# Shared products of the end blocks on 64 or on 128 rows of the array

## The chip, the cores and the metric

The kernel runs on one core of a Trainium2 chip. Its time is the device time of one execution in microseconds (us); a lower time is better. The core has five engines that run side by side and wait for each other through semaphores: TensorE (PE in the profile, its weight loads PEld), VectorE (DVE), ScalarE (ACT), GpSimd (POOL) and SyncE (SP). DMA queues move data between device memory and the on-chip memory. TensorE multiplies a stationary operand, loaded as weights, with a moving operand that streams through its array of 128 rows by 128 columns. It can also be used as smaller arrays: a product named 64*32 in the profile uses 64 rows and 32 columns, one named 64*128 uses 64 rows and all columns, and one named 128*128 uses the whole array.

## The reference

The first part is attention with a block mask, for 4 batches, 8 heads, 768 tokens of 64 values, in blocks of 32 tokens (24 blocks). The second part is a feed-forward network on the attention's output.

```python
scores = scale * np.matmul(q, k.transpose(0, 1, 3, 2))
mask = np.abs(blk_i - blk_j) <= window                  # window = 1
mask = mask | (blk_i == 0) | (blk_j == 0) | (blk_i == n_blocks - 1) | (blk_j == n_blocks - 1)
for qb in range(n_blocks):
    for kb in sampled_blocks[qb]:                       # 3 random blocks
        mask[qb * block:(qb + 1) * block, kb * block:(kb + 1) * block] = True
scores = np.where(mask, scores, -1000000000.0)
attn = softmax(scores)
x = np.matmul(attn, v)                                  # to [3072 tokens, 512]
h = x @ w_in                                            # [3072, 2048]
out = gelu(h) @ w_out                                   # [3072, 512]
```

So a block of queries sees its own block and its two neighbours, three sampled blocks, and the two end blocks (block 0 and block 23). Query blocks 0 and 23 see all blocks; they are called dense here. All other query blocks need the values of both end blocks, each weighted with its own probabilities.

## The kernel before

The kernel works through eight units, two for each batch (`Unit`, L300). A unit holds three quads of four query blocks. The first unit of a batch (quads 1, 2, 0) holds also the two dense blocks; the second one (quads 3, 4, 5) has only sparse blocks. Quads 0 and 5 have three sparse blocks, since their fourth is dense; the other two groups of a unit have four.

All work is written out in one order by hand (`manual_schedule`), and every engine runs its instructions in that order. For each unit there is a stage for the first feed-forward product (`ffn1_step`, L502), and after it an attention stage for the next unit (`attention`, L562) into which the pieces of the second feed-forward product of the unit before are put as filling (`ffn2_pieces`, L524, L529; the lists of numbers that are given to `attention` say how many pieces go into which round). In a round of the attention stage the order is: scores on TensorE (`scores`, L335), row maxima on VectorE (L360 for sparse, L363 for dense blocks), exponentials on ScalarE (L377, L381), a transpose of the probabilities in 32x32 squares on VectorE (`turned`, L394 into the tile pT, L399 into ptd), and when a group is done, the weighed values on TensorE (`values`, L407), the division by the sums on VectorE (`divided`, L467), a transpose on TensorE (`outputs`, L486, tile tx) and a copy to the feed-forward input xT on ScalarE (L494).

On the on-chip memory's partitions the eight heads stand in pairs: rows 0 to 63 hold two heads and rows 64 to 127 two others, in each of two groups G. `values` works for one half (one G) at a time. In the tile kv a block's values stand with 32 rows for a head, so that one product over 64 rows adds two heads at once; each head has its own 65 columns (64 values and a one that gives the sum), and the columns of the other head of the pair hold zeros. The two pairs h = 0 and h = 1 go to two places of the accumulator av.

For a group of four query blocks a half has 52 products. The first four are the shared products of the end blocks (L434 and L457): the weights are the probabilities of all four query blocks (128 columns) for the end block, the moving operand is the end block's values (130 columns), once for the rows 0 to 63 and once for the rows 64 to 127, first for block 0 and then for block 23. They are 64*128 products. The other 48 are of one query block each (64*32): own block, neighbours and sampled blocks, whose values were gathered into gb beforehand (`gather`, L296). The weights wait for pT from VectorE.

The gathers for the next unit run during the first feed-forward stage. For a new batch they are on VectorE (L739 to L741), then comes a hold on POOL (`hold_loads`, L158: a copy of one value that makes POOL wait) and the rest of the gathers on POOL. For the first batch's second unit the hold stands at L719. `value_list` (L191) works out once, in three scratch rows of 72 numbers, which sampled blocks count.

Of the kernel before, what the change touches and what calls it, by code (L numbers as in the profile page):

```python
# [10 lines left out]
F32 = mybir.dt.float32  # L11
BF16 = mybir.dt.bfloat16
# [8 lines left out]
def kernel(  # L21
# [58 lines left out]
    ptd = const.tile([P, 2, NE, 2, BL, 2], BF16, name="ptd")  # L80
    xTs = [const.tile([P, KIN, UT], BF16, name=f"xT{i}") for i in range(2)]
    g = const.tile([P, KOUT, UT], BF16, name="g")
    mark = const.tile([1, 1], BF16, name="mark")
    junk = const.tile([1, 1], BF16, name="junk")

# [9 lines left out]
    def sampled(i, r):  # L95
        c0 = GW * (i // 3) + 4 * BW + DW * (i % 3) + BW * r
        return gb[:, c0:c0 + BW]
# [58 lines left out]
    def hold_loads(x):  # L156

        nc.gpsimd.tensor_copy(mark, x)  # L158
# [30 lines left out]
    vf = const.tile([1, NB, NR], I32, name="vf")  # L189

    def value_list():  # L191
        rf = const.tile([1, NB, NR], F32, name="rf")
        inv = const.tile([1, NB, NR], F32, name="inv")
        tmp = const.tile([1, NB, NR], F32, name="tmp")
        nc.vector.tensor_copy(rf, raw[:, :, :, 0])
        nc.vector.tensor_tensor(tmp, rf, jrow, op=ALU.subtract)
        nc.vector.tensor_tensor(tmp, tmp, tmp, op=ALU.mult)
        nc.vector.tensor_scalar(inv, tmp, 1.0, None, op0=ALU.is_le)
        for c in (0.0, float(NB - 1)):
            nc.vector.scalar_tensor_tensor(out=inv, in0=rf, scalar=c, in1=inv,  # L200
                                           op0=ALU.is_equal, op1=ALU.max)
        for a, c in ((1, 0), (2, 1)):
            w = NR - a if c == 0 else 1
            nc.vector.tensor_tensor(tmp[:, :, 0:w], rf[:, :, a:a + w],
                                    rf[:, :, c:c + 1].to_broadcast([1, NB, w]), op=ALU.is_equal)
            nc.vector.tensor_tensor(inv[:, :, a:a + w], inv[:, :, a:a + w], tmp[:, :, 0:w],
                                    op=ALU.max)
        nc.vector.scalar_tensor_tensor(out=vf, in0=inv, scalar=float(NB), in1=rf,
                                       op0=ALU.mult, op1=ALU.max)
# [56 lines left out]
    def gather_fixed(kT, place, copy=None, part=None):  # L266

        copy = copy or nc.vector.tensor_copy
        groups = gb.rearrange("p (g x) -> p g x", x=GW)
        js = sorted(place)  # L270
        runs = [[j for j in js if place[j] - j == c] for c in sorted({place[j] - j for j in js})]
        for run in runs if part != 1 else ():
            i0 = place[run[0]]
            assert i0 % 3 == 0
            for lane in range(min(3, len(run))):
                m, g0 = len(range(lane, len(run), 3)), i0 // 3
                c0, j = BW + KC * lane, run[0] + lane - 1
                copy(
                    groups[:, g0:g0 + m, c0:c0 + 3 * BW].rearrange("p g (w c) -> p g w c", c=BW)[:, :, :, 0:KC],
                    kT[:, j:j + 3 * m, :].rearrange("p (g w) c -> p g w c", w=3))  # L280
        if part == 0:
            return
        at = slice(min(place.values()) // 3, max(place.values()) // 3 + 1)
        n = at.stop - at.start
        copy(groups[:, at, 0:3 * KC].rearrange("p g (l c) -> p g l c", c=KC),
             kT[:, None, 0:1, :].to_broadcast([P, n, 3, KC]))
        copy(  # L287
            groups[:, at, 4 * BW:GW].rearrange("p g (l x) -> p g l x", x=DW)[:, :, :, NR * BW:DW],
            kT[:, None, NB - 1:NB, :].to_broadcast([P, n, 3, KC]))

    def gather(unit, js, at, c0=0, c1=BW, engine=None):

# [114 lines left out]
    def values(unit, grp, half):  # L407
        kv = kvs[unit.b % 2]
        if half == 0:

            pool, tag = (psA, "A") if grp == units[0].ends[len(units[0].rounds) - 1] else (psV, "V")
            st[grp, "av"] = pool.tile([P, 2, 512], F32, name="av", tag=tag)
        av = st[grp, "av"]
        if grp[0][0] == "d":
            pv = ptd.rearrange("p g c x q e -> p g c (x q) e")
            for c in range(NB // 2 * half, NB // 2 * (half + 1)):
                for G in range(2):
                    for h in range(2):
                        rows = slice(64 * h, 64 * h + 64)
                        c0 = KC + V2 * G  # L420
                        nc.tensor.matmul(av[64 * G:64 * G + 64, h, 0:V2],
                                         lhsT=pv[rows, G, c // 2, :, c % 2],
                                         rhs=kv[rows, c, c0:c0 + V2],
                                         start=(c == 0), stop=(c == NB - 1))
            n, m = 4, 2
        else:
            slots = [j for rnd in grp for j in rnd[1]]
            G = half
            c0 = KC + V2 * G
            pv = st[grp, "pt"][:, G].rearrange("p c (q e) -> p c q e", e=2)  # L430

            work = []
            if len(slots) == 4:
                work += [(0, 4, c, kv[:, blk, c0:c0 + V2]) for c, blk in ((0, 0), (7, NB - 1))]  # L434
            for c in range(1, 7) if work else range(8):
                for s, j in enumerate(slots):
                    if c in (0, 7):
                        blk = 0 if c == 0 else NB - 1
                        if abs(blk - j) <= 1:
                            continue  # L440
                        src = kv[:, blk, c0:c0 + V2]
                    elif c < 4:
                        src = kv[:, j - 2 + c, c0:c0 + V2]
                    else:
                        src = sampled(unit.place[j], c - 4)[:, c0:c0 + V2]
                    work.append((s, 1, c, src))
            fresh, left = set(range(len(slots))), {s: 0 for s in range(len(slots))}
            for s, w, _, _ in work:
                for x in range(s, s + w):
                    left[x] += 1  # L450
            for s, w, c, src in work:
                at = range(s, s + w)
                for x in at:
                    left[x] -= 1
                for h in range(2):
                    rows = slice(64 * h, 64 * h + 64)
                    nc.tensor.matmul(av[32 * s:32 * (s + w), h, V2 * G:V2 * G + V2],  # L457
                                     lhsT=pv[rows, c % 4, BL * s:BL * (s + w), c // 4], rhs=src[rows],
                                     start=s in fresh, stop=left[s] == 0)
                fresh -= set(at)  # L460
            n, m = len(slots), 4
            if half:
                st.pop((grp, "pt"))
        if half:
            st[grp, "av"] = av, n, m
# [237 lines left out]
    for n, unit in enumerate(units):  # L703
# [11 lines left out]
        for s in range(KOUT // 2):  # L715
            ffn1_step(n, 2 * s)
            if s == 0:
                if n == 0:
                    hold_loads(sampled(nxt.place[J1[7]], NR - 1)[0:1, BW - 1:BW])  # L719
                    gather(nxt, J1[8:], others, engine=nc.gpsimd)  # L720
                    ones(1)
                elif fresh and b + 2 < B:
                    xT, t0 = column[b, unit.groups[-2][0]]
                    hold_loads(xT[0:1, 0, t0:t0 + 1])
                    load_by_token(qn, q, b + 2)
                    load_by_token(kn, k, b + 2)
                    turn_queries(b + 2)
                elif nxt is not None and not fresh:
                    if b + 1 < B:
                        turn_keys()  # L730
                        hold_loads(sampled(nxt.place[J1[7]], NR - 1)[0:1, BW - 1:BW])
                        load_values(b + 1)
                    gather(nxt, J1[8:], others, engine=nc.gpsimd)
            if s == 7 and nxt is not None:
                table(AF.Exp)
                if n > 0 and not fresh and b + 1 < B:
                    next_keys(b + 1)
            if fresh and s == 0:
                gather_fixed(keys(b + 1), nxt.place)  # L739
                gather(nxt, J0[3:9], known)  # L740
                gather(nxt, J0[:3], known)  # L741
                hold_loads(sampled(nxt.place[J0[2]], NR - 1)[0:1, BW - 1:BW])
                gather(nxt, J0[9:], others, engine=nc.gpsimd)
        filler = ffn2_pieces(n)
# [51 lines left out]
```

## Time and profile before

| what | value |
|---|---|
| time, median of 3 runs | 290.33 us (289.07 to 290.67) |
| span of the profiled execution | 288.1 us |
| TensorE busy in the span | 263.8 us (92%) |
| VectorE, ScalarE busy | 207.6 us, 207.7 us (72% each) |
| GpSimd busy | 101.2 us (35%) |
| share of TensorE in the chain that ended last | 65% |
| second feed-forward product, L529 | 336 products, 87.0 us busy |
| first feed-forward product, L507 | 512 products, 85.0 us busy |
| weighed values, L457 | 2400 products, of which 128 are shared ones of the end blocks |

The profile is of one execution, and its time as the runs count it isn't given beside its span; the median of the runs is 2.2 us above the span. Busy time of TensorE counts a product from its issue to its last result, so products that follow each other overlap, and a group's mean is a latency. What a product costs in a row of products is the distance from one start to the next. The timeline gives starts to 0.01 us; a row there joins instructions of one kind that follow each other, and the count behind its x covers those of the window that was asked for. In a row with several products the last one starts at the row's end less the latency of one.

### The profile page before, as it was taken

To read this page: it belongs to the slowest core of one execution; us is meant where nothing else is said; L and a number is where in the kernel's file an instruction comes from. 1 tells how busy PE (TensorE), PEld (TensorE's weight loads), DVE (VectorE), ACT (ScalarE), POOL (GpSimd) and SP (SyncE) were. 2 spreads that over 40 slices of the span, in tenths; PEclk is the share of its full clock that TensorE was granted. 3 is DMA by queue.
4 is the path that set the end of the run, shared out by engine and by line. 5 is a ranking of instruction groups with operands and counts; after the bars stand their busy time and mean duration, and the time that the engine had idled before them with its cause. 6 is when DMAs were issued, how large, how long until landed. Compare 5 with 4: busy or idle time off the path is not lost.

```text
span 288.1 us, 11491 instructions
## 1 busy us (share of the span) xinstructions
PE 263.8 (92%) x4918; PEld 143.4 (50%) x4918; DVE 207.6 (72%) x476; ACT 207.7 (72%) x379; POOL 101.2 (35%) x209
## 2 busy tenths in 40 slices
PE   1798799998998999999998999899999999899994
PEld 1624555445553555445544556355535555356543
DVE  7599787866888967598998876798749796871000
ACT  8779746875868966796778865986688766966611
POOL 8788944308792001920990004900120032000000
PEclk9999999999999999999999999999999999999999
DMA  6997399919999116991997119930101110111002
GB/s 103 168 91 118 50 197 205 206 49 113 91 165 151 39 41 149 81 69 41 102 151 116 65 51 134 84 50 35 40 0 41 39 41 0 39 42 39 0 36 74
DMA packets 72981, 23.80 MB, mean 83 GB/s; under 512 B 63073, under 2 KB 69474, under 8 KB 72930
## 3 DMA queue, kind: packets, MB, share of 16 engines
q0 software_dynamic: 56912, 13.64, 77.8%
q1 hardware_dynamic: 16018, 9.44, 11.9%
q8 instruction: 38, 0.62, 0.9%
q14 instruction: 13, 0.11, 0.2%
HBM read 27.26 MB, written 6.29 MB: 116 GB/s over the span
## 4 chain that ended last, share of the span: by engine, by line
PE 65%; ACT 19%; DVE 7%; issue 3%; DMA 3%; POOL 1%; ACTq 0%; POOLq 0%
PE hp L507 27%; PE op L529 18%; PE av L457 10%; ACT pp L377 8%; ACT L405 4%; PE sc L335 3%; ACT g L510 3%; DMA qn<-in_q_dram 3%; DVE nm L360 3%; PE tx L486 2%; PE av L558 2%; PE op L558 2%; ACT pp L381 2%; PE pt L227 2%; DVE nm L363 1%
## 5 line engine op out<-in xcount | busy, mean ns | idle before, releaser
L529 PE MATMUL op<-w_out_sb,g 128*128 128x512 bf16 x336 | 87.0, 381 | 0.5 <-ACT os L515 0.3
L507 PE MATMUL hp<-xT,w_in_sb 128*128 128x384 bf16 x512 | 85.0, 326 | 0.8 <-ACT xT L494 0.4
L377 ACT ACTIVATE pp<-sc,nm 128x256 bf16<-128x256 f32 x176 | 75.3, 542 | 7.7 <-DVE nm L360 7.5
L510 ACT ACTIVATE g<-hp 128x768 bf16<-128x768 f32 (+1 forms) x72 | 52.1, 738 | 31.4 <-PE hp L507 31.4
L507 PEld LDWEIGHTS <-w_in_sb 128*128 128x128 bf16 x512 | 50.0, 98 | 36.0 <-issue 3.1
L360 DVE TENSOR_REDUCE nm<-sc 128x4 f32<-128x1024 f32 (+1 forms) x48 | 52.9, 1107 | 7.2 <-PE sc L335 7.2
L296 POOL COPY gb<-kv 128x388 bf16 (+1 forms) x87 | 36.5, 474 | 26.5 <-DVE gb L287 24.1
L529 PEld LDWEIGHTS <-g 128*128 128x128 bf16 x336 | 28.2, 97 | 34.6 <-issue 11.6
L296 DVE COPY gb<-kv 128x388 bf16 x177 | 39.9, 305 | 1.2 <-DMA qn<-in_q_dram 1.2
L457 PEld LDWEIGHTS <-pT 64*32 64x32 bf16 (+1 forms) x2400 | 26.1, 91 | 19.8 <-DVE pT L394 7.9
L394 DVE STREAM_TRANSPOSE pT<-pp 128x512 f32<-128x512 f32 (+1 forms) x48 | 31.5, 656 | 5.9 <-ACT pp L377 5.7
L457 PE MATMUL av<-kv,pT 64*32 64x130 bf16 (+1 forms) x1344 | 28.2, 220 | 3.0 <-DVE pT L394 1.1
L158 POOL COPY mark<-gb 1x1 bf16<-1x1 bf16 x6 | 1.1, 178 | 80.2 <-DVE gb L296 80.2
L335 PE MATMUL sc<-gb,qT 64*32 64x256 bf16 x704 | 19.1, 274 | 5.7 <-ACT pp L377 3.7
L134 POOL DMA_DIRECT2D kv<-in_v_dram x32 | 22.9, 724 | 1.8 <-DMA qn<-in_q_dram 1.1
L494 ACT COPY xT<-tx 128x512 bf16<-128x512 bf16 (+1 forms) x32 | 13.6, 450 | 13.1 <-PE tx L486 13.1
L335 PEld LDWEIGHTS <-qT 64*32 64x32 bf16 x832 | 11.2, 90 | 21.4 <-issue 14.6
L381 ACT ACTIVATE pp<-sc,nm 128x768 bf16<-128x768 f32 x16 | 17.1, 1104 | 4.9 <-DVE nm L363 4.9
L363 DVE TENSOR_REDUCE nm<-sc 128x1 f32<-128x768 f32 x16 | 15.0, 944 | 7.8 <-PE sc L335 7.3
L457 PE MATMUL av<-gb,pT 64*32 64x130 bf16 x1056 | 19.8, 220 | 0.7 <-issue 0.7
L405 ACT ACT_TABLE_LOAD x15 | 19.2, 1283 | 0.3
L476 DVE TENSOR_TENSOR xh<-av,rec 128x512 bf16<-128x512 f32 (+2 forms) x28 | 18.3, 652 | 1.0
(75 smaller groups left out, 225.3 us busy)
## 6 DMA issues: line engine op xcount, KB each, us to landing
out_dram<-os SPq DMA_DIRECT2D x23, 256.0 KB, 2.0
kv<-in_v_dram POOLq DMA_DIRECT2D x32, 96.0 KB, 6.5
w_out_sb<-in_moe_w_out_dram POOLq DMA_DIRECT2D x2, 1024.0 KB, 13.4
kn<-in_k_dram POOLq DMA_DIRECT2D x4, 384.0 KB, 11.2
qn<-in_q_dram POOLq DMA_DIRECT2D x4, 384.0 KB, 12.8
qn<-in_q_dram POOLq DMA_DIRECT2D x12, 128.0 KB, 5.4
kn<-in_k_dram POOLq DMA_DIRECT2D x12, 128.0 KB, 5.9
w_in_sb<-in_moe_w_in_dram POOLq DMA_DIRECT2D x2, 512.0 KB, 10.2
```

Source lines behind the costliest of these rows:

```text
L134: nc.gpsimd.dma_start(out=kvs[b % 2][32 * hh:32 * hh + 32, 0:NB, c0:c0 + D], in_=v[b, h].rearrange("(n p) d -> p n d", p=BL))
L296: (engine or nc.vector).tensor_copy(sampled(unit.place[j], r)[:, None, c0:c1], src[:, bass.ds(at[j][r], 1), :])
L335: nc.tensor.matmul(o, lhsT=qT[rows, j // 4, pr, BL * (j % 4):BL * (j % 4) + BL], rhs=rhs(rows, pr), start=True, stop=True)
L360: nc.vector.tensor_reduce(out=nm[:, 0:2 * n].rearrange("p (g j) -> p g j", g=2), in_=A4[:, :, 0:n, :], op=ALU.max, axis=AX.X, negate=True)
L377: nc.scalar.activation(at[:, x // n, x % n], A[:, a:a + 256].rearrange("p (e c k) -> p e c k", e=2, k=BL), AF.Exp, bias=nm[:, x:x + 1])
L381: nc.scalar.activation(pp[:, 0:S].rearrange("p (c k e) -> p c e k", e=2, k=BL), A[:, 0:S].rearrange("p (c e k) -> p c e k", e=2, k=BL), AF ...
L394: nc.vector.transpose(pt.rearrange("p g c x -> p (g c) x")[:, :, 64 * s:64 * (s + n)].bitcast(F32), pp[:, 0:512 * n].bitcast(F32).rearrang ...
L405: nc.scalar.activation(junk, zero[0:1, 0:1], func)
L457: nc.tensor.matmul(av[32 * s:32 * (s + w), h, V2 * G:V2 * G + V2], lhsT=pv[rows, c % 4, BL * s:BL * (s + w), c // 4], rhs=src[rows], start ...
L507: nc.tensor.matmul(hp[:, i, 0:T], lhsT=w_in_sb[:, ki, (m + i) * P:(m + i + 1) * P], rhs=xTs[n % 2][:, ki, 0:T], start=(ki == 0), stop=(ki ...
L510: nc.scalar.activation(g[:, m + i[0]:m + i[1], 0:T], hp[:, i[0]:i[1], 0:T], AF.Gelu)
L529: nc.tensor.matmul(op, lhsT=g[:, m, t * P:(t + 1) * P], rhs=w_out_sb[:, m, :], start=(m == 0), stop=(m == KOUT - 1))
```

## The change

The shared products of the end blocks keep their weights and their number, but each one uses all 128 rows. For that a new tile `ends` holds the values of the two end blocks twice: in its first copy the rows 64 to 127 are zero, in its second the rows 0 to 63. A product with the first copy adds the pair h = 0 alone, one with the second copy the pair h = 1. The four products of a half are 128*128 products with 130 columns, in the same order as before. The first unit keeps the old form.

The tile is filled by `apart`: two copies of 64 rows for a batch. For the first batch POOL does them ahead of the hold in the first feed-forward stage of unit 0, with two memsets that write the zeros once; for the three other batches VectorE does them behind the gathers of the new batch. The three scratch rows of `value_list` get no tiles of their own any more and lie in the tile g, which is first written later.

```diff
+    ends = const.tile([P, 2, 2, 2 * V2], BF16, name="ends")
...
-        rf = const.tile([1, NB, NR], F32, name="rf")
-        inv = const.tile([1, NB, NR], F32, name="inv")
-        tmp = const.tile([1, NB, NR], F32, name="tmp")
+        rf, inv, tmp = [g[0:1, i, 0:2 * NB * NR].bitcast(F32).rearrange("o (j r) -> o j r", r=NR)
+                        for i in range(3)]
...
+    def apart(b, engine):
+        for h in range(2):
+            rows = slice(64 * h, 64 * h + 64)
+            engine.tensor_copy(ends[rows, h], kvs[b % 2][rows, 0:NB:NB - 1, KC:BW])
...
-            if len(slots) == 4:
+            if len(slots) == 4 and unit is not units[0]:
+                for i, c in enumerate((0, 7)):
+                    for h in range(2):
+                        nc.tensor.matmul(av[:, h, V2 * G:V2 * G + V2],
+                                         lhsT=pv[:, c % 4, 0:P, c // 4],
+                                         rhs=ends[:, h, i, V2 * G:V2 * G + V2],
+                                         start=(i == 0), stop=False)
+            elif len(slots) == 4:
                 work += [(0, 4, c, kv[:, blk, c0:c0 + V2]) for c, blk in ((0, 0), (7, NB - 1))]
-            for c in range(1, 7) if work else range(8):
+            for c in range(1, 7) if len(slots) == 4 else range(8):
...
-            fresh, left = set(range(len(slots))), {s: 0 for s in range(len(slots))}
+            shared = len(slots) == 4 and unit is not units[0]
+            fresh = set() if shared else set(range(len(slots)))
+            left = {s: 0 for s in range(len(slots))}
...
                 if n == 0:
+                    for h in range(2):
+                        nc.gpsimd.memset(ends[64 * h:64 * h + 64, 1 - h], 0.0)
+                    apart(0, nc.gpsimd)
                     hold_loads(sampled(nxt.place[J1[7]], NR - 1)[0:1, BW - 1:BW])
...
                 gather(nxt, J0[:3], known)
+                apart(b + 1, nc.vector)
                 hold_loads(sampled(nxt.place[J0[2]], NR - 1)[0:1, BW - 1:BW])
```

## The prediction

> **What bounds the kernel now.** I read the page first (span and busy shares), then the stretches of the attention stages, then the groups kept apart by shape, then the timeline around single products.
>
> ```profile
> span 288.1 us, 11491 instructions
> ...
> PE 263.8 (92%) x4918; PEld 143.4 (50%) x4918; DVE 207.6 (72%) x476; ACT 207.7 (72%) x379; POOL 101.2 (35%) x209
> ```
>
> The runs of before have a median of 290.33 us (289.07 to 290.67); the profiled execution spans 288.1, so some 2.2 us lie around the span, and I leave them as they are. The next view has one row for each stretch in which an attention stage has its weighed values (us, then busy time and instructions of PE, PEld, DVE, ACT, POOL, then the granted clock).
>
> ```profile
> 94.75:107.98 13.23, 13.21 (x387) 7.36 (x388) 10.67 (x24) 10.00 (x24) 0.00 (x0) 1.00 0.12 43
> 124.10:137.30 13.20, 13.19 (x399) 7.12 (x399) 11.90 (x22) 10.20 (x20) 0.58 (x2) 1.00 0.45 52
> 157.35:170.59 13.24, 13.22 (x387) 7.37 (x388) 10.66 (x24) 10.02 (x24) 0.00 (x0) 1.00 0.12 44
> ```
>
> TensorE is busy 13.21 of 13.23 us: in these stages TensorE's own order is the path, and a nanosecond added to or taken from it is a nanosecond of the result. The clock is 1.00, so nothing here is about throttling. The dense stage (first row) comes back as the third: the schedule repeats, so one stage can stand for three.
>
> **The products that change.** All shared products of the end blocks are this group; 32 halves of four products each.
>
> ```profile
> L457 PE MATMUL av<-kv,pT 64*128 64x130 bf16 x128 | 9.2, 223 | 1.1 <-DVE pT L394 1.1
> ```
>
> The four halves of the first unit keep the old form, so 28 halves (112 products) change. The 223 ns is the latency of one, not what one costs. The cost is in the starts, here of a half that follows another half:
>
> ```profile
> 101.49 0.42 PE L457 MATMUL av<-gb,pT 64*32 64x130 bf16 x24
> ...
> 101.85 0.29 PE L457 MATMUL av<-kv,pT 64*128 64x130 bf16 x4
> ...
> 102.07 0.36 PE L457 MATMUL av<-kv,pT 64*32 64x130 bf16 x22
> ```
>
> From the first shared product to the first small one (64*32) pass 0.22 us. Next, what full-array products (128*128) cost. The tx products have 128 columns, ours 130.
>
> ```profile
> 103.91 0.39 PE L486 MATMUL tx<-identity,xh 128*128 128x128 bf16 x4
> ...
> 104.13 0.59 PE L529 MATMUL op<-w_out_sb,g 128*128 128x512 bf16 x2
> ```
>
> ```profile
> 98.21 0.28 PE L486 MATMUL tx<-identity,xh 128*128 128x128 bf16 x2
> ...
> 98.41 0.47 PE L457 MATMUL av<-kv,pT 64*128 64x130 bf16 x12
> ```
>
> Four tx products and the step into the next product of the same shape take 0.22, so 0.055 a step, each with its own weight load. Two tx products and the step into another shape take 0.20: 0.09 more than two steps. So a change of shape costs 0.09 us. This is where the old form loses: 0.22 is one step for a pair, one step for the second pair, and 0.09 to the small shape; four products in two steps means that the two row halves run at once.
>
> The new form does the four one behind the other: 4 x 0.056 (130 columns for 128) and 0.09 to the small shape, 0.32. Against 0.22 that is 0.10 more for each half, **28 x 0.10 = +2.7 us** (2.7 to 2.8 by the rounding of the rows), wherever the half stands. The Trainium skill, "TensorE: Matmul & The Clock Gate", section "Why this matters for your kernels", speaks against this change in the same sense: a product with few rows takes as long as one with 128, and the gain of short ones is that they run beside each other. By that rule the padding buys nothing in the array; the trace agrees (0.22 for four short products with the exit, 0.22 for four full ones without it).
>
> **What is saved is the way in.** Behind a full-array product the shape no longer changes. The FFN steps and one such entry:
>
> ```profile
> 272.89 3.45 PE op L558 x16
> ```
>
> ```profile
> 124.95 0.81 PE L529 MATMUL op<-w_out_sb,g 128*128 128x512 bf16 x3
> 125.69 0.40 PEld L457 LDWEIGHTS <-pT 64*128 64x128 bf16 x25 [0.42 <-issue]
> ```
>
> Sixteen FFN products in 3.45 are 0.216 a step. The third product of the row at 124.95 starts at 125.38, and the shared one starts with its load at 125.69: 0.31, so 0.095 can go. Over the 28 halves the timeline has 18 behind an FFN product (first 56.90, last 255.44), 6 behind tx products (first 65.91, last 223.61) and 4 behind small products (101.85, 164.45, 227.05, 256.19). The last four save nothing. If the other 24 saved all, the gain would be 24 x 0.094 = 2.3 us, and the whole +0.5.
>
> They don't save all, since the product must also have its weights, pT, from VectorE's transpose.
>
> ```profile
> 95.56 0.70 DVE L394 STREAM_TRANSPOSE pT<-pp 128x512 f32<-128x512 f32 x1
> ...
> 96.35 0.34 PEld L457 LDWEIGHTS <-pT 64*128 64x128 bf16 x14 [0.42 <-DVE pT L394]
> ```
>
> ```profile
> 100.33 0.70 DVE L394 STREAM_TRANSPOSE pT<-pp 128x512 f32<-128x512 f32 x1
> ...
> 101.09 0.35 PEld L457 LDWEIGHTS <-pT 64*128 64x128 bf16 x17 [0.43 <-DVE pT L394]
> ```
>
> At 101.09 the weights are loaded 0.06 after the transpose ended (101.03): this half already waits for pT and the change of shape is hidden under that wait; it saves nothing, and so do its two repeats (163.70, 226.29). At 96.35 the transpose ended at 96.26, 0.09 before; the half can start only 0.03 earlier. Such are 96.35, 158.95, 221.55 (0.09 to 0.10 before) and 130.24, 192.85, 255.44 (0.13): together 3 x 0.06 + 3 x 0.02 = 0.24 of the saving is lost. With 3 x 0.095 for the three that wait, 0.53 goes. A first step after a wait or a change of shape is 0.01 longer (0.24 against 0.22 is what four tx products take behind small ones), for these nine and the four behind small products 0.13.
>
> **Copies that feed the products.** Two copies (64 rows of 520 values each) and two memsets on POOL for the first batch, two copies on VectorE for each of the three further batches.
>
> ```profile
> L296 DVE COPY gb<-kv 128x388 bf16 x177 | 39.9, 305 | 1.2 <-DMA qn<-in_q_dram 1.2
> ...
> L278 DVE COPY gb<-kv 128x1152 bf16<-128x1152 bf16 x7 | 5.2, 742 | 0.0
> ```
>
> Bounds for one are 0.3 (fewer values) and 0.74 (more than twice as many); by the nearest, 388 values in 0.305, I take 0.4, so 0.8 a batch. They stand behind the gathers of the next unit (L296); the next in VectorE's queue is the first maximum of the next stage, and for that ScalarE waits with the exponentials.
>
> ```profile
> 149.20 1.98 DVE L363 TENSOR_REDUCE nm<-sc 128x1 f32<-128x768 f32 x2 [0.31 <-PE sc L335]
> ```
>
> ```profile
> 149.64 1.28 ACT L405 ACT_TABLE_LOAD   x1
> ...
> 151.04 2.05 ACT L381 ACTIVATE pp<-sc,nm 128x768 bf16<-128x768 f32 x2
> ```
>
> VectorE idles 0.31 there in the third batch, the tightest of the three. The maxima come 0.5 late, the first at 150.7; ScalarE needs it at 151.04, behind its table load. Covered, with 0.3 to spare; price zero. Without that cover it would be 0.5 once, or 1.2 with the dear copies (2 x 0.74 - 0.31). The copies also wait for the products of the stage before, which is over at 137.30 (second stretch above), 11.6 earlier; POOL's hold (L158) waits for the gather ahead of them.
>
> ```profile
> 38.64 0.69 POOL L103 DMA_DIRECT2D qn<-in_q_dram  x1
> ...
> 47.29 0.18 POOL L158 COPY mark<-gb 1x1 bf16<-1x1 bf16 x1 [7.95 <-DVE gb L296]
> ```
>
> POOL idles 7.95 where its four instructions go; even at 0.74 each they take 3. Zero. The three scratch rows moved into g are the same instructions on other addresses, and g is first written after 38 us. Zero.
>
> **Sum.** +2.74 - 2.26 + 0.53 + 0.13 = **+1.1 us**; the span goes to 289.3, and the median to 291.5 us (+0.4%). Its own range is +0.5 (every saving comes) to +1.8 (one rounding unit of 0.01 on each half, way in and wait).
>
> **Rivals.** (1) Slower: the weight loads show. The loads of pT step over two values at a time; those of tx, which I took as the model, don't. A load lasts 98 ns.
>
> ```profile
> L486 PEld LDWEIGHTS <-xh 128*128 128x128 bf16 x72 | 5.2, 98 | 3.5 <-issue 0.3
> ```
>
> If the next load could not run under a product, a step would be 0.098 for 0.056: 28 x 3 x 0.042 = 3.5 more, 294.9 us. Against it: in the half at 101.85, whose loads have the same stride, the second pair comes within a step. The Trainium skill, same page, section "Back-to-back issue gap", gives about 81 ns for sustained loads and products of 128 columns; by it the sum would be some 2 us higher (an estimate, 28 x 3 x 25 ns), while the tx row here has 55.
>
> (2) Slower: VectorE's copies come out dear and the cover breaks, 1.2 in the third batch: 292.7. For it: only 0.31 idle there; against it: the table load.
>
> (3) No change: TensorE gets slack back at the stage ends, 290.3. For it: the stages begin with chains of ScalarE; against it: 13.21 of 13.23.
>
> (4) Faster: the way from the full array to the small shape is short. The price 0.09 is from tx products going to 64*128; with short products and the small shape behind them no quoted row shows it. If small weights were let in at once, 28 x 0.09 = 2.5 go, and the whole becomes -1.4: 288.9. It decides for faster where that change costs under 0.05. Against it stand long products:
>
> ```profile
> 53.88 0.60 PE L529 MATMUL op<-w_out_sb,g 128*128 128x512 bf16 x2
> 54.41 0.41 PE L335 MATMUL sc<-gb,qT 64*32 64x256 bf16 x16
> ```
>
> The second of them starts at 54.10 (0.38 before its end), and the small ones come 0.31 later, a step of 0.216 and again 0.09.
>
> **How the numbers follow.** About 0.5%, 1.45 us, is what a measurement of this kernel can tell from no change. Forecast 0.65: with the scatter of runs 0.41 within the bound, 0.24 over it. Rival 1 has 0.10, slower. Rival 2 has 0.07: 0.05 slower, 0.02 within. Rival 3 has 0.09: 0.08 within, 0.01 faster. Rival 4 has 0.09, at the bound: 0.06 faster, 0.03 within. That is 0.07 faster, 0.54 same, 0.39 slower. The range 289.2 to 293.6 leaves out rivals 1 and 4 (0.19); it is the forecast's own (290.8 to 292.2) with the scatter of the runs, and rivals 2 and 3.
>
> **What would show it.** The group at 64*128 keeps 16 products and a 128*128 group of 112 with 128x130 appears. The timeline of a half shows starts 0.055 to 0.06 apart and the first small product 0.32 behind the first shared; behind an FFN product with early pT the first comes 0.216 after it. The halves at 101.1 and 101.85 lose 0.1 each. A dense stage grows by about 0.3, a sparse one by up to 0.1 (the last, with a half behind a small product, by 0.2). Steps of 0.08 or more are rival 1, an exit under 0.05 is rival 4, and a first exponential later than its table load is rival 2.

## The result and the profile after

The changed kernel takes 293.26 us (median; 292.49 to 294.31) against 290.2 before, a ratio of 1.0111 with a 95% interval of 1.0088 to 1.0135: slower by 1.1%, some 3.1 us. The forecast was 291.5, within half a per cent of before, and the range reached to 293.6: the time lies inside, near the upper end, and 1.8 us over the likeliest value. Ratios, here and below, are of the fast executions alone, so that one can differ a little from the quotient of two medians.

The four executions aren't alike. Two have a mean granted clock of 0.999 and 0.997 and took 292.49 and 292.53 us; the other two have 0.993 and 0.991 and took 293.99 and 294.31. The profile is of the first, whose span, 290.7, is 1.8 us less than its time; with the same 1.8 the profiled execution of the kernel before (span 288.1) took some 289.9 us, an estimate, and not the median.

The first lines of the page, the stretches of the attention stages that answer to the three shown before, and the instructions that touch the new tile `ends`:

```profile
span 290.7 us, 11497 instructions
...
PE 264.5 (91%) x4918; PEld 147.3 (51%) x4918; DVE 211.2 (73%) x482; ACT 208.3 (72%) x379; POOL 104.5 (36%) x213
```

```profile
94.17:107.72 13.55, 13.50 (x387) 7.81 (x388) 10.67 (x24) 10.11 (x24) 0.00 (x0) 1.00 0.12 42
123.84:137.10 13.26, 13.24 (x399) 7.71 (x399) 11.92 (x22) 10.23 (x20) 0.58 (x2) 1.00 0.41 51
159.12:172.65 13.53, 13.50 (x387) 7.80 (x388) 10.64 (x24) 10.09 (x24) 0.00 (x0) 1.00 0.12 42
```

```profile
L441 PE MATMUL av<-ends,pT x112: 217/220/233, 56.3 to 258.8; 128*128 128x130 bf16 x112
L294 DVE COPY ends<-kv x6: 277/294/2926, 85.6 to 209.9; 64x520 bf16<-64x520 bf16 x6
L734 POOL MEMSET ends<- x2: 532/544/557, 38.7 to 39.2; 64x520 bf16 x2
L294 POOL COPY ends<-kv x2: 839/850/862, 39.8 to 40.7; 64x520 bf16<-64x520 bf16 x2
```

The dense stages went from 13.23 to 13.55 and from 13.24 to 13.53, the sparse one from 13.20 to 13.26: the products cost what was forecast. The last view (durations are minimum, median, maximum in ns) has the surprise: four of VectorE's six copies took about 0.29 us, one took 0.65 and one 2.93. The last two stand side by side in the third batch. The timelines of VectorE, POOL and ScalarE around that copy:

```profile
140.25 8.00 DVE L301 COPY gb<-kv 128x388 bf16 x27
148.16 3.59 DVE L294 COPY ends<-kv 64x520 bf16<-64x520 bf16 x2
151.78 1.82 DVE L368 TENSOR_REDUCE nm<-sc 128x1 f32<-128x768 f32 x2
```

```profile
148.72 0.18 POOL L159 COPY mark<-gb 1x1 bf16<-1x1 bf16 x1
148.83 2.77 POOL L301 COPY gb<-kv 128x388 bf16 x6
```

```profile
149.44 1.28 ACT L410 ACT_TABLE_LOAD   x1
150.74 0.20 ACT L410 ACTIVATE junk<-zero 1x1 bf16<-1x1 bf16 x1
152.78 2.07 ACT L386 ACTIVATE pp<-sc,nm 128x768 bf16<-128x768 f32 x2 [1.83 <-DVE nm L368]
```

VectorE's second copy starts at 148.82, POOL's first one of the gather at 148.83, and VectorE's copy ends at 151.75, after POOL's sixth (151.60). By these starts VectorE's copy was 0.01 us ahead, and yet it was the one that waited: a start in the profile isn't to a hundredth the moment that decides. The first maximum waits behind it in VectorE's queue, and ScalarE waits 1.83 us for that maximum, where before it had gone on right behind its table load. In the second and the fourth batch VectorE's second copy started 0.04 and 0.46 us ahead of POOL's first one and took 0.29; in the second batch it was POOL's first copy that got longer, 0.62 for 0.51.

Where the time came from is seen best at one mark in every stage, the first weight load of the first feed-forward product. The table has the shift of that mark against the kernel before in us, worked out from the traces; runs are described below. What counts is the step from one column to the next, since the first columns differ by what happened ahead of the first mark.

| mark before at | 37.53 | 74.92 | 107.61 | 137.50 | 170.21 | 200.11 | 232.81 | 262.11 |
|---|---|---|---|---|---|---|---|---|
| changed kernel | -0.52 | -0.58 | -0.26 | -0.20 | +2.06 | +2.11 | +2.42 | +2.57 |
| hold behind the copies | +1.97 | +1.24 | +1.56 | +1.61 | +1.92 | +1.97 | +2.27 | +2.43 |
| products alone | +0.04 | -0.29 | +0.03 | +0.09 | +0.39 | +0.43 | +0.74 | +0.89 |
| copies alone | -0.27 | -0.28 | -0.06 | -0.07 | +2.97 | +2.96 | +2.97 | +2.95 |
| both halves' products first | +0.33 | +0.16 | -0.08 | -0.25 | -0.52 | -0.71 | -0.96 | -1.31 |

In the changed kernel the dense stages add 0.32, 2.26 and 0.31, the sparse ones 0.06, 0.05 and 0.15. The middle one is 1.94 over its sisters. So in this execution 1.2 us are the products and 1.9 us the copy that stood.

That this makes the same 3.1 us as the difference of the medians is partly chance. The profiled execution as a whole is only 2.6 us longer than that of the kernel before (spans of 290.7 and 288.1), because its first mark comes 0.52 earlier. The median lies between two executions 2.3 us over the kernel before and two that are 3.8 and 4.1 over it, at the lower clock.

### The profile page after: what moved, and what is told of

The parts are those of the page before. It is cut to its first block, busy times and chain, and to the rows that moved or that the text cites. A ratio compares the mean times of both kernels' runs of the same rounds, so it can differ in the third digit from the quotient of the medians.

```text
span 290.7 us, 11497 instructions
## 1 busy us (share of the span) xinstructions
PE 264.5 (91%) x4918; PEld 147.3 (51%) x4918; DVE 211.2 (73%) x482; ACT 208.3 (72%) x379; POOL 104.5 (36%) x213
## 4 chain that ended last, share of the span: by engine, by line
PE 62%; ACT 17%; DVE 12%; issue 3%; DMA 3%; POOL 1%; DVEq 0%; ACTq 0%; POOLq 0%
PE hp L521 24%; PE op L543 17%; PE av L471 8%; ACT pp L382 8%; ACT L410 4%; PE sc L340 3%; PE av L441 3%; DMA qn<-in_q_dram 3%; DVE nm L365 2%; ACT g L524 2%; DVE gb L301 2%; PE tx L500 2%; PE av L572 2%; ACT pp L386 2%; PE op L572 2%
## 5 line engine op out<-in xcount | busy, mean ns | idle before, releaser
L301 DVE COPY gb<-kv 128x388 bf16 x177 | 39.3, 299 | 2.8 <-DMA qn<-in_q_dram 2.7
L471 PEld LDWEIGHTS <-pT 64*32 64x32 bf16 (+1 forms) x2288 | 22.9, 91 | 10.7 <-DVE pT L399 3.6
L471 PE MATMUL av<-kv,pT 64*32 64x130 bf16 (+1 forms) x1232 | 22.1, 219 | 2.5 <-DVE pT L399 1.1
```

Of the source, the lines that this page charges most:

```text
L301: (engine or nc.vector).tensor_copy(sampled(unit.place[j], r)[:, None, c0:c1], src[:, bass.ds(at[j][r], 1), :])
```

## The experiments

My theory from here (the port theory of the expectations): VectorE's copies and POOL's copies can't run at the same time on a path to memory that they share, the port; the one that comes second waits; and POOL, which had six copies queued, kept VectorE's single copy out until all six were done. Rivals: the copy is dear by itself in that batch, beside the loads in flight; or the products cost the whole 3.1.

**The hold behind the copies.** POOL may begin only when both copies are done.

```diff
                 apart(b + 1, nc.vector)
-                hold_loads(sampled(nxt.place[J0[2]], NR - 1)[0:1, BW - 1:BW])
+                hold_loads(ends[64:65, 1, 1, 2 * V2 - 1:2 * V2])
```

> The changed kernel, but POOL's hold in front of its gather waits for the second copy into ends and not for VectorE's last gather, so POOL's copies can't start beside VectorE's. Port theory (the 2.9 us of the second copy in the third batch are a wait for POOL's six copies): both copies take 0.3 to 0.65 us, the first maximum of that stage comes at most 0.5 us late and ScalarE's exponential starts right behind its table load again; 1.9 us of the loss go, 1.2 stay with the products: 291.4 us, ratio to before 1.004. Rival, dear copies (the copy is slow by itself in that batch, beside the loads): copy 2.9 us as before, POOL's gather 2.4 us later, time 293.3, ratio 1.011.

Measured: 291.49 us, ratio 1.0053 (1.0039 to 1.0067). VectorE, then POOL, in the third batch:

```profile
149.96 0.96 DVE L294 COPY ends<-kv 64x520 bf16<-64x520 bf16 x2
150.95 1.84 DVE L368 TENSOR_REDUCE nm<-sc 128x1 f32<-128x768 f32 x2
153.77 0.58 DVE L404 STREAM_TRANSPOSE ptd<-pp 128x384 f32<-128x384 f32 x1 [0.98 <-ACT pp L386]
```

```profile
151.06 0.18 POOL L159 COPY mark<-ends 1x1 bf16<-1x1 bf16 x1 [0.54 <-DVE ends L294]
151.30 2.77 POOL L301 COPY gb<-kv 128x388 bf16 x6
```

The loads ran beside the copies as before, and both copies together took 0.96. So they aren't dear by themselves; POOL's gather made one so. A small part of the rival holds: the first copy took 0.65 here too, where POOL was issuing loads (in this run until 150.52), against 0.28 in the second and the fourth batch. And it isn't every instruction of VectorE that waits: the two maxima ran beside POOL's six copies in 1.84 us. VectorE then waits 0.98 for ScalarE as it did in the kernel before: the cover holds. In the table the step of 1.94 is gone, and from the second mark to the last 1.19 us are left.

**The copies alone.** The changed kernel with the old products; nobody reads `ends`.

```diff
-            if len(slots) == 4 and unit is not units[0]:
+            if False:
...
-            shared = len(slots) == 4 and unit is not units[0]
+            shared = False
```

> The kernel before with the tile ends and all its copies, but with the old products; ends is read by nobody. Port theory: +1.9 us (292.1, ratio 1.007) if POOL wins the start in the third batch as it did there, with a copy of 2.9 us in that batch; about 0 if VectorE wins it, with no copy over 0.7. Rival, dear copies: +1.9 in any case. Rival, products cost all of it: 0.0.

Measured: 292.14 us, ratio 1.0085 (1.0063 to 1.0106). The copies and, below, the wait in the third batch and what follows it (us, then busy time of PE, PEld, DVE, ACT, POOL, then the granted clock):

```profile
L294 DVE COPY ends<-kv x6: 277/293/2929, 85.9 to 210.7; 64x520 bf16<-64x520 bf16 x6
```

```profile
151.00:155.20 4.20, 1.87 (x24) 0.65 (x22) 3.86 (x5) 2.13 (x3) 0.72 (x2) 1.00 1.53 193
155.25:158.66 3.41, 3.08 (x67) 1.71 (x67) 2.81 (x4) 2.87 (x8) 0.00 (x0) 0.50 0.19 31
```

The two starts lay the same 0.01 us apart here, and the copy took 2.93. The jump at the mark is 3.0 us and not 1.9: behind the wait, in which TensorE had little to do, TensorE was granted half its clock for 3.41 us, and that fits the other 1.1. No such stretch lies in the other two dense stages (what the 0.22 in the second batch is stays open). The Trainium skill, "TensorE: Matmul & The Clock Gate", section "Part 1: The HAM clock gate", says that the clock falls to half after an idle window of some 3.4 us and rises after a busy one; the length here, 3.41, agrees. TensorE wasn't idle for a whole window, though: in the 3.41 us before the drop (151.84 to 155.25) it was busy for 1.20. Nor does this wait always bring a drop, or every drop come from it. In the profiled execution of the changed kernel TensorE's longest wait there was the same (2.33 us) and the clock stayed up; with the hold behind the copies, where the wait is gone, TensorE was at half clock from 36.2 to 39.6, behind a stop of 1.44 us that has no releaser in the profile (the two make that run's 1.97 at the first mark). So a wait on VectorE can cost TensorE more than its length, but where the two slower executions of the changed kernel lost their clock isn't shown.

**The products alone.** No copies for the later batches, so that those add the end blocks' values of the first batch.

```diff
-                apart(b + 1, nc.vector)
```

> The changed kernel without the copies of the three later batches: ends keeps the end blocks of the first batch, so later batches add the wrong end values. The array's work is that of the change. Theory (+0.10 for each of 28 halves, 0.095 back where the way in is free): +1.2 us, 291.4, ratio 1.004. Rival, products cost all: +3.1, ratio 1.011. Rival, copies cost all: 0.

Measured: 291.40 us, ratio 1.0056 (1.0034 to 1.0078). The table has +0.89 - (-0.29) = 1.18 us from the second mark to the last, in steps of 0.32, 0.30 and 0.31 at the dense stages: the products' 1.2 and nothing else.

**The copies on ScalarE.** The copy is ScalarE's own instruction there.

```diff
...
-                apart(b + 1, nc.vector)
+                apart(b + 1, nc.scalar)
```

> The changed kernel with the copies of the three later batches on ScalarE instead of VectorE, at the same place of the program. Port theory: ScalarE doesn't share the port with POOL, so its copies take under 1 us whatever POOL does, ScalarE waits for TensorE between its activations there, and only the products' 1.2 us stay: 291.1 to 291.4, ratio 1.004. Rival, dear copies beside the loads: ScalarE's copies take 2 to 3 us in the third batch and the time stays at 293, ratio 1.011.

Measured: 292.39 us, ratio 1.0076 (1.0048 to 1.0105). ScalarE's copies, and ScalarE and TensorE at the second batch's feed-forward stage:

```profile
L294 ACT COPY ends<-kv x6: 609/616/624, 78.3 to 206.3; 64x520 bf16<-64x520 bf16 x6
```

```profile
78.32 1.26 ACT L294 COPY ends<-kv 64x520 bf16<-64x520 bf16 x2
79.60 1.51 ACT L524 ACTIVATE g<-hp 128x768 bf16<-128x768 f32 x2
```

```profile
75.56 4.37 PE L521 MATMUL hp<-xT,w_in_sb 128*128 128x384 bf16 x24
80.47 6.66 PE L521 MATMUL hp<-xT,w_in_sb 128*128 128x384 bf16 x40 [0.54 <-ACT g L524]
```

ScalarE's copies took 0.61 or 0.62 us in all six. The first four ran beside POOL's issues of loads, which had made a copy of VectorE's 0.65 for 0.28, the last two while POOL was idle: ScalarE isn't slowed by POOL there, as the port theory has it. Beside POOL's gather, which came later (from 86.3, 150.4 and 210.7), this run doesn't try them. My price for the place was wrong. The copies stand among the first activations of the stage, whose results free the two accumulators that TensorE fills in turn; two copies are 1.23 us, ScalarE's slack a step is less, and TensorE waits (0.54 in this row). The feed-forward stage grew by 0.7 us in each of the three batches, together a little more than the 1.94 that POOL's wait had cost once. In time the two are alike: 292.39 here, 292.5 in the two executions of the changed kernel that kept their clock.

**A longer gather.** POOL's six copies behind the hold are done twice.

```diff
-                gather(nxt, J0[9:], others, engine=nc.gpsimd)
+                for _ in range(2):
+                    gather(nxt, J0[9:], others, engine=nc.gpsimd)
```

> The changed kernel, but POOL's gather behind the hold is done twice in each new batch (12 copies instead of 6, the second six write the same again). Port theory with POOL keeping the port as long as it has copies queued: VectorE's second copy in the third batch takes 2.9 + 2.7 = 5.6 us, and the time grows by 2.7 over the changed kernel, to 296, ratio 1.020. Port theory with the port given up after a fixed time or number of copies: the copy stays at 2.9 us and the time at 293. Rival, dear copies: the copy stays at 2.9 us.

Measured: 297.69 us, ratio 1.0279 (1.0232 to 1.0326).

```profile
L294 DVE COPY ends<-kv x6: 280/293/5660, 86.0 to 214.8; 64x520 bf16<-64x520 bf16 x6
```

```profile
149.32 0.18 POOL L159 COPY mark<-gb 1x1 bf16<-1x1 bf16 x1
149.44 5.50 POOL L301 COPY gb<-kv 128x388 bf16 x12
```

The copy took 5.66 us, 2.73 more, as POOL's gather got 2.73 longer (5.50 for 2.77). So the copy waits for the whole run of POOL's copies, not for one of them and not for a fixed time; in the changed kernel, with the copies alone and here it ended 0.15 us after the last of them. POOL's copies leave no gap between them in the profile: each starts 0.45 us after the one before it and lasts 0.50. The time grew by 1.7 us more than that, as did the step at the mark in the profiled execution (6.63 for 2.25): the clock was at half for 6.83 us behind this wait (155.0 to 161.8). Here the drop isn't a matter of the execution: all four have a mean clock of 0.986 or 0.987.

**Both halves' products first.** If passes and changes of shape set the price, the old 64*128 products should be gathered, not widened. Here a group's first half does the shared products of both halves, and its second half has only small products.

```diff
-                work += [(0, 4, c, kv[:, blk, c0:c0 + V2]) for c, blk in ((0, 0), (7, NB - 1))]
-            for c in range(1, 7) if work else range(8):
+                if half == 0:
+                    for i, (c, blk) in enumerate(((0, 0), (7, NB - 1))):
+                        for g2 in range(2):
...
+                            for h in range(2):
+                                rows = slice(64 * h, 64 * h + 64)
+                                nc.tensor.matmul(av[:, h, V2 * g2:V2 * g2 + V2],
+                                                 lhsT=pg[rows, c % 4, 0:P, c // 4],
+                                                 rhs=kv[rows, blk, KC + V2 * g2:KC + V2 * g2 + V2],
+                                                 start=(i == 0 and g2 == 0), stop=False)
+            for c in range(1, 7) if len(slots) == 4 else range(8):
...
```

> The kernel before with the old 64*128 products, but a group's first half does the shared products of both halves (eight in a row), and its second half starts with the small ones. Theory (the array pays for passes and for changes of shape): ten separated second halves save 0.22 and pay 0.11 in the first half, four adjacent ones save 0.37 and pay 0.11, together 2.1 us less: 288.1, ratio 0.993. Rival, the changes of shape are hidden by the ring through ScalarE and VectorE: 0. Rival, a longer first half delays the scores that follow: slower by up to 14 x 0.11 = 1.5.

Measured: 288.70 us, ratio 0.9963 (0.9943 to 0.9983). Faster than both kernels, by about half of what I expected. A second half behind an FFN product:

```profile
127.24 0.38 PE L539 MATMUL op<-w_out_sb,g 128*128 128x512 bf16 x1
127.55 0.36 PE L467 MATMUL av<-kv,pT 64*32 64x130 bf16 x24
```

The small products start 0.31 behind the FFN product, at the moment when the shared ones used to start, so the 0.22 of the shared products is gone here. In the table the kernel gains 1.47 us from the second mark to the last, 0.24 to 0.27 at a dense stage (0.37 by the prices of the expectation: 0.11 for a separated second half, 0.26 for an adjacent one), 0.17 and 0.19 at a sparse one (0.22) and 0.35 at the last (0.37), and 0.17 before the second mark. So the profile shows 1.64 of the 2.1 us, and the medians 1.2.

**All products small.** The other way to save the change of shape: no 64*128 products at all.

```diff
-            if len(slots) == 4:
-                work += [(0, 4, c, kv[:, blk, c0:c0 + V2]) for c, blk in ((0, 0), (7, NB - 1))]
```

> The kernel before, but the shared products are taken apart: each end block is multiplied for one query block at a time, 16 products of 64*32 for the four of 64*128, among the other 48. Theory (passes and changes of shape set the price): eight small products run at once, so 16 are two passes of 0.06 to 0.07 us, as many as the two pairs took, and the change from 64*128 to 64*32 (0.09) is gone; each of the halves on TensorE's path gets 0.08 to 0.1 shorter, 28 of them 2.2 to 2.8 us: 287.3 to 287.9, ratio 0.991. Rival, the rate of issue binds: 12 more loads and products at 8 to 9 ns a pair are 0.1 us more for each half, and nothing is left: 290, ratio 1.000.

Measured: 296.73 us, ratio 1.0186 (1.0128 to 1.0244): slower, where I expected faster by 0.9%. The first rows are a half of the kernel before with the scores behind it, the second the same half here, the third an interruption:

```profile
96.35 0.58 PE L457 MATMUL av<-kv,pT 64*128 64x130 bf16 x28
96.75 0.42 PE L457 MATMUL av<-gb,pT 64*32 64x130 bf16 x24
96.96 0.45 PE L335 MATMUL sc<-gb,qT 64*32 64x256 bf16 x16
```

```profile
100.43 0.42 PE L455 MATMUL av<-kv,pT 64*32 64x130 bf16 x32
100.69 0.42 PE L455 MATMUL av<-gb,pT 64*32 64x130 bf16 x24
100.89 0.28 PE L455 MATMUL av<-kv,pT 64*32 64x130 bf16 x8
100.95 0.45 PE L335 MATMUL sc<-gb,qT 64*32 64x256 bf16 x16
```

```profile
172.66 0.29 PE L455 MATMUL av<-gb,pT 64*32 64x130 bf16 x9 [0.87 <-issue]
```

```profile
40.91 0.29 PE L484 MATMUL tx<-identity,xh 96*128 96x96 bf16 x3 [2.65 <-issue]
```

The half itself did get shorter, from 0.61 to 0.52 us: the array behaved as I had it. But TensorE stood still several times with nothing that the profile shows to wait for ("issue"): 1.55 us at 30, 2.65 at 38 and 0.5 to 0.9 three times later, together 6.1 us against 1.5 in the kernel before. The kernel has 384 more products, each with its weight load, and one of the two queues that bring instructions moved 41 packets instead of 38. The stops that ended at 31.3, 40.9, 164.4, 172.7 and 236.4 each ended 2.3 to 2.6 us after such a packet was begun, and so did the two of the kernel before (35.3 and 60.7). That fits a sequencer that ran out of instructions, but no run here takes the fetch away, so the cause stays open. A stretch of 3.41 us at half the clock, from 41.6, came on top.

## Why the prediction was right or wrong

**The passes, +0.10 for each half: right.** The timeline of the changed kernel at the half that follows another half, and at one behind an FFN product with an early pT:

```profile
101.48 0.40 PE L441 MATMUL av<-ends,pT 128*128 128x130 bf16 x4
101.81 0.36 PE L471 MATMUL av<-kv,pT 64*32 64x130 bf16 x24
```

```profile
125.13 0.38 PE L543 MATMUL op<-w_out_sb,g 128*128 128x512 bf16 x1
125.35 0.39 PE L441 MATMUL av<-ends,pT 128*128 128x130 bf16 x4
```

```profile
125.67 0.37 PE L471 MATMUL av<-kv,pT 64*32 64x130 bf16 x24
```

From the first shared product to the first small one pass 0.33 and 0.32 (0.22 before), forecast 0.32. The way in is 0.22 behind the FFN product (0.31 before). The strided weights cost nothing, the way out to the small shape is the 0.09 of the model, and both rivals of that part (loads that show, a short way out) are out. The Trainium skill's 81 ns for a load and product of this size ("TensorE: Matmul & The Clock Gate", section "Back-to-back issue gap") doesn't hold here: the steps are 0.057, which is the 0.40 of a row of four less the 0.23 of one product, over three.

**The lost saving where pT is late: right.** The dense stages, in which three of four halves save little, grew by 0.30 to 0.32 (forecast 0.3), the sparse ones by 0.05 to 0.06, the last by 0.15. The products' sum was forecast as 1.1 and measured as 1.18 and 1.19 in the two runs that leave the copies' wait out. These two figures hold 24 of the 28 halves; the other four lie ahead of the second mark, have their weights early, and should cost as much as they save.

**POOL's copies and memsets, priced at zero: right.** They took 2.8 us of an idle stretch of 7.95.

**VectorE's copies, priced at zero: this step failed.** The prediction said of them: "Covered, with 0.3 to spare; price zero." It took a copy's own duration (0.4) and looked for what is late behind it in its own queue; in the third batch the two took 0.65 and 2.93, and ScalarE waited 1.83 us for the first maximum. It had named what POOL does at that moment only to say that the hold "waits for the gather ahead of them", as a reason that POOL isn't delayed. That should have been read the other way round: with VectorE's gather over, POOL is free to begin its six copies just when VectorE's two are to run. These are the hold and the six in the third batch of the kernel before:

```profile
149.03 0.18 POOL L158 COPY mark<-gb 1x1 bf16<-1x1 bf16 x1 [0.55 <-DVE gb L296]
149.16 2.77 POOL L296 COPY gb<-kv 128x388 bf16 x6
```

How near the two come depends on more. In the changed kernel's third batch POOL was still issuing loads when the gather ended (148.25); its hold ran at 148.72 without a wait. Beside the loads VectorE's first copy took 0.65 for 0.28, and that is what brought the second one to 148.82; with 0.28 it would have started some 0.38 ahead of POOL's first (an estimate from the same rows), as it started 0.04 and 0.46 ahead in the batches where nothing waited. The timeline of before had a sign of such sharing, VectorE's gather beside POOL's loads in the third batch and without them in the last:

```profile
140.91 7.98 DVE L296 COPY gb<-kv 128x388 bf16 x27
202.86 4.68 DVE L296 COPY gb<-kv 128x388 bf16 x27
```

It was not used.

**Rival 2 is what happened in that place,** the third batch, by breaking the same cover; but with another mechanism, and 1.94 in place of 1.2, since it took its price from a dear copy that stands alone. Together with the products that gives 3.1 us by the marks of the profiled execution. The Trainium skill, "SBUF — State Buffer", section "Who interferes with whom", has the rule that was missing: a VectorE copy that uses both of its ports and a GpSimd instruction exclude each other, and the one that starts second waits in full. The trace agrees that one of the two waits; which ports the copy used no run shows, and the longer gather shows that the wait is for all that POOL had queued and not for one instruction.

**That the time lies in the range is partly luck.** The forecast's own range ended at 292.2. The rest, up to 293.6, was given for the scatter of the runs and for rivals of which none happened as it was told. The measured 1.1% is also clear of the half per cent within which the likeliest value lay, and "nothing here is about throttling" didn't stay true: two of the four executions have a lower clock, which no term of the sum allowed for.

## What to carry to other kernels

A product on half the array's rows that has a partner on the other half costs half a pass; widening it with zeros buys at most one change of shape (0.09 us here) and pays with passes (0.06 each), so it is better to bring products of one shape together than to give them another shape. An instruction added to an engine with slack has to be checked against every engine that becomes free at about the same moment and may share its way to memory, not only against what stands behind it in its own queue. Where an experiment adds instructions to the engine that sets the pace, look for stops without a releaser before believing the saved time.

## What the runs showed that was not expected

VectorE's copy waited for POOL's whole queue of copies: 2.93 us for six, 5.66 for twelve, against 0.29 alone; VectorE's maxima beside the same six copies didn't wait. A wait of some 2 us on VectorE halved TensorE's granted clock for one window of 3.41 us in one of two profiled executions with that wait, and for 6.83 us behind the longer one; the cost on top of the wait was 1.1 and 1.7 us. But a stretch at half clock came without such a wait too. And 384 more small products, with a half shorter by 0.09 us, made the kernel 1.9% slower, with 6.1 us of stops of TensorE whose cause stays open.
